# Gated mix of sliding-window attention and a Mish MLP on one core: the softmax in two halves, the gate's sums on VectorE, two chunks of the first projection pass by pass, and the causal bound added by GpSimd

## The chip, the core and the metric

The kernel runs on one core of a Trainium2 chip. A core has TensorE (PE, matrix multiply into PSUM), VectorE (DVE), ScalarE (ACT), GpSimd (POOL) and SyncE (SP, which here issues all DMA transfers). They run beside each other and are tied by semaphores; each works through its own instructions in order. The metric is the device time of one execution in microseconds. Before the change it is 655.41 us (median of three runs, 655.38 to 655.86).

## The reference: what is computed

x has 2048 rows of 640 numbers, all in f32. There are 32 heads of 20, a window of eight keys two rows apart, and an MLP of width 1728:

```
g    = sigmoid(sum(x * gate_w))                                    one number a row
q,k,v = x @ wqkv, in 32 heads
o    = softmax(q . k[row - 0, -2, ..., -14] * 20**-0.5) . v        keys before row 0 count as -1e9
a    = o @ wo
b    = mish(x @ w1 + b1) @ w2
out  = g * a + (1 - g) * b
```

## The kernel before: tiling, stages, order

**Matmuls in three parts.** Every f32 operand is split into a high half (ScalarE, L309) and a low half (a subtraction on VectorE or GpSimd, L312; "ANY" lets either take it). Three matmuls, high by high, high by low and low by high (L343 to L345), replace one f32 matmul. A split operand lives in a "pair" buffer; there are 21 of them, given out in a fixed order, and 14 of the 20 x chunks, wq, w2 and the MLP's activations share them. Raw loads go through seven "raw" and four "hb" buffers; three "w" buffers hold w1.

**Rows and units.** Row 16p + i sits on partition p in slot i. P = 0 or 1 picks every second slot (eight each), since keys lie two rows apart. Attention goes in eight units u = 2 hq + P: hq is one of four groups of eight heads. For each unit `qkv` (L448) projects eight slots: per slot five chunks of 128 input columns, three matmuls each, 120 matmuls of NCOL columns a unit. The columns are 160 each of q, k and v, 16 of the rest of w1, and in the units with hq = 0 two more that hold gate_w, so 498 columns there and 496 later. ScalarE evacuates a bank with L436 (k and v), L438 (q) and L441 (w1's rest), and in units 0 and 1 with one more copy (L443) of the gate's sum into zt. `make_gates` turns zt into the sigmoid. Unit 0 goes chunk by chunk over its first four slots, as the loads arrive: the three matmuls of slot 0, of slot 1, and so on.

**Attention** (L375) runs on VectorE with k, v and q in SBUF (three stores kvq0 to kvq2, used in turn; unit 7 has kvq2). For pairs of slots 6, 4, 2, 0: the product with eight shifted keys (L380, "qk") and its sum over 20 (L383). Then once for all eight slots: the causal bound by a min with `bound` on partition 0 (L387), maximum (L389), subtraction (L390), Exp on ScalarE (L391, with a table load), sum (L392), reciprocal (L393), times the gate (L394), shares pw (L395). Then for each pair of slots the product with v (L400) and three halving additions (L404, L405, L407), and after each two pairs a transpose (L351) whose result is spilled to DRAM. Keys from other partitions come by two halo copies a unit (L480, DMA). The evacuation of unit u into a store waits until unit u - 2 has freed the slot.

**The MLP.** `mlp1` (15 matmuls a bank) fills TensorE between the units; its Mish output goes to DRAM. `mlp2(tb)`, for four blocks tb of 512 columns, takes fourteen steps fc of 15 matmuls (10 in the last); each step needs one pair of activations, and in mlp2(0) one of w2 as well. The results, times 1 - g, are kept, and `wo_out` adds the attention's output projection at the end.

**What sets the order.** No order is written out by hand. `Plan` records every operation as a task with an engine, an estimated time, a rank (SOON, NEXT, LATER; smaller first), tasks it waits for and buffers it takes; `run` (L88) plays them through and issues each engine's instructions in the order that comes out. A change of any estimate can move instructions. Two rules matter here: VectorE takes an "ANY" split during the score products only if it has been ready for 2 us, and GpSimd takes splits only in stretches after a "qk" product unless a task has rank below 0.

Of the kernel before, what the change touches and what calls it, by code (L numbers as in the profile page):

```python
# [8 lines left out]
F32 = mybir.dt.float32  # L9
# [11 lines left out]
FC = 13  # L21
FR = F - FC * 128
RQ = FR // NQ
NCOL = 3 * QF + RQ + 2
ROW = 2 * QF
BIG = 1e9
WARM = 9
# [157 lines left out]


@with_exitstack
def kernel(ctx: ExitStack, tc: tile.TileContext, x, wq, wo, w1, b1, w2, out):
    nc = tc.nc
    scale = DH ** -0.5  # L190
    V, G, A = nc.vector, nc.gpsimd, nc.scalar
# [104 lines left out]
    def consts_g():  # L296
        for i in range(2):
            G.memset(KV[i][0:1, 0:7], 0.0)

        G.memset(bound, 3e38)  # L300
# [74 lines left out]
    def attention(u, P, hq, ready, gates):  # L375
        kv, q, r = KV[UNIT[u]], Q[UNIT[u]], LATER
        prev = last_att[0]
        for s0 in range(6, -1, -2):
            def mul(s0=s0):
                return V.tensor_tensor(pr, window(kv, s0, 0), q[:, s0:s0 + 2, None, :].to_broadcast([128, 2, W, QF]), op=OP.mult)  # L380

            def red(s0=s0):
                V.tensor_reduce(lg_w[:, s0:s0 + 2], pr.rearrange("p s w (h d) -> p s w h d", d=DH), op=OP.add, axis=AX.X)  # L383

            prev = add("DVE", 2850, mul, [prev] + ready[s0], rank=r, kind="qk")
            prev = add("DVE", 2830, red, [prev], rank=r, kind="qk sum")
        prev = add("DVE", 560, lambda: V.tensor_tensor(lg[0:1, 0:7, :, 0:7], lg[0:1, 0:7, :, 0:7],  # L387
                   bound[:, :, None, :].to_broadcast([1, 7, HQ, 7]), op=OP.min), [prev, cg], rank=r)
        prev = add("DVE", 690, lambda: V.tensor_reduce(mx, lg, op=OP.max, axis=AX.X), [prev], rank=r)  # L389
        prev = add("DVE", 700, lambda: V.tensor_tensor(lg, lg, mx[:, :, :, None].to_broadcast([128, 8, HQ, W]), op=OP.subtract), [prev], rank=r)  # L390
        prev = add("ACT", 630 + 2 * TABLE, lambda: A.activation(lg, lg, AF.Exp, scale=scale), [prev], rank=-1)  # L391
        prev = add("DVE", 690, lambda: V.tensor_reduce(sm, lg, op=OP.add, axis=AX.X), [prev], rank=r)  # L392
        prev = add("DVE", 560, lambda: V.reciprocal(sm, sm), [prev], rank=r)  # L393
        prev = add("DVE", 230, lambda: V.tensor_tensor(sm, sm, gate[:, P, :, None].to_broadcast([128, 8, HQ]), op=OP.mult), [prev] + gates, rank=r)  # L394
        prev = add("DVE", 700, lambda: V.tensor_tensor(pw.rearrange("p s w h -> p s h w"), lg, sm[:, :, :, None].to_broadcast([128, 8, HQ, W]), op=OP.mult), [prev], rank=r)  # L395
        for s0 in range(6, -1, -2):
            def mul(s0=s0):
# [5 lines left out]
            prev = add("DVE", 2850, mul, [prev], rank=r, kind="pv")  # L403
            prev = add("DVE", 1510, lambda: V.tensor_tensor(pr[:, :, 0:4], pr[:, :, 0:4], pr[:, :, 4:8], op=OP.add), [prev], rank=r)  # L404
            prev = add("DVE", 850, lambda: V.tensor_tensor(pr[:, :, 0:2], pr[:, :, 0:2], pr[:, :, 2:4], op=OP.add), [prev], rank=r)  # L405

            prev = add("DVE", 515, lambda s0=s0: V.tensor_tensor(q[:, s0:s0 + 2], pr[:, :, 0], pr[:, :, 1], op=OP.add), [prev], rank=r)  # L407
            if s0 % 4 == 0:
                ot = plan.buf("ot", lambda: at.tile([128, QF // 32, 4, 32], F32, name="ot"))
                prev = add("DVE", 830, lambda s0=s0, ot=ot: turn(ot.t, q[:, s0:s0 + 4], QF // 32), [prev], rank=r, take=[ot])  # L410
                tb = 2 * P + (s0 == 0)
                spilled[tb, hq] = turned_out(lambda tb=tb: o_d[tb][hq * QF:(hq + 1) * QF], lambda ot=ot: ot.t, [prev], [ot])
                for s in range(s0, s0 + 4):
                    freed[u, s] = [prev]
        att_end[u] = prev
        last_att[0] = prev

# [11 lines left out]
    def qkv_part(ps, P, hq, i, kc, n):  # L429
        xs = tuple(X[2 * P + i // 4, kc].t[:, j, (i % 4) * 128:(i % 4 + 1) * 128] for j in range(2))  # L430
        mm3(ps.t[:, :n], xs, tuple(WQ[hq, kc].t[:, j, :n] for j in range(2)), kc == 0, kc == KC - 1)

    def qkv_evac(u, P, hq, i, ps, done):
        kv, q, s = KV[UNIT[u]], Q[UNIT[u]], 4 * (1 - i // 4) + i % 4
        before = freed.get((u - 2, s), []) if u < 7 else [zero2[0]]
# [4 lines left out]
        def rest():  # L440
            A.activation(hx[:, P, i, hq], ps.t[:, 3 * QF:3 * QF + RQ], AF.Copy)  # L441
            if hq == 0:
                A.activation(zt[:, P, s:s + 1], ps.t[:, NCOL - 2:NCOL - 1], AF.Copy)  # L443

        c = add("ACT", 170 * (2 if hq == 0 else 1), rest, [b], rank=SOON, hold=[ps])
        return a, b, c

    def qkv(u, P, hq):  # L448
        n = NCOL if hq == 0 else NCOL - 2
        kv = KV[UNIT[u]]  # L450
        ev = {}
        pss = [ps_buf() for _ in range(8)]
        if u == 0:
            last = warmed
            for kc in range(KC):
                for i in range(4):
                    last = pe_add(3 * mm_ns(n), lambda i=i, kc=kc: qkv_part(pss[i], P, hq, i, kc, n),
                               [last] + X[0, kc].ready + WQ[hq, kc].ready, take=[pss[i]] if kc == 0 else [],
                               hold=[pss[i], X[0, kc], WQ[hq, kc]])
# [24 lines left out]
        if hq == 0:  # L484
            gates[P] = [make_gates(P, [ev[i][2] for i in range(8)])]
        attention(u, P, hq, ready, gates[P])

    hxd = {0: [], 1: []}
    g_done = {}

    def make_gates(P, after):
        def run():
# [190 lines left out]
        X[tb, kc] = load_pair(lambda: x[tb, kc], eng, wide=True, home=x_home[:, i] if i < 6 else None, **k)  # L683

    def wq_in(hq, kc, eng, **k):
        n = NCOL if hq == 0 else NCOL - 2
        WQ[hq, kc] = load_pair(lambda: wq[hq, kc][:, :n], eng, n=n, wide=hq == 0, **k)

    def w1_in(fc, eng="ANY"):
# [7 lines left out]
        x_in(1, kc, "DVE")  # L697
    for fc in range(2):
        w1_in(fc)
    for tb in (2, 3):  # L700
        for kc in range(KC):
            x_in(tb, kc, "ANY")

    todo = [(fc, t) for fc in (0, 1) for t in (0, 1)] + [(fc, t) for fc in (0, 1) for t in (2, 3)]
    todo += [(fc, t) for fc in range(2, 10) for t in range(4)]
# [84 lines left out]
```

## Time and profile before

| | |
|---|---|
| median of the runs | 655.41 us (655.38 to 655.86) |
| profiled execution | 655.15 us |
| its span, first to last instruction | 653.4 us |
| mean granted TensorE clock | 0.999 |
| matmuls | 2869 |
| DMA | 82.35 MB, mean 126 GB/s |

TensorE's stages, by the starts of the first matmul of each:

| stage | starts at, us |
|---|---|
| warm-up matmuls | 1.20 |
| unit 0 | 4.70 |
| mlp1 | 32.50 |
| unit 1 | 59.72 |
| mlp1 | 86.91 |
| unit 2 | 114.14 |
| units 3, 4, 5 | 171.14, 228.14, 285.14 |
| units 6 and 7 | 342.14 |
| mlp2(0) and what follows | 394.94 |

VectorE's first score product of the eight units starts at 33.23, 93.82, 147.66, 210.83, 267.35, 324.04, 383.54 and 460.52 us; its last transpose of attention at 526.05.

How to read it: a row of the timeline is start, duration, engine, line, operation, output and input, shape, count, and in brackets the idle time before it with what ended it. A row of a group has the shape and count, then busy time and mean ns of one, then the idle time in front of the group. A matmul's duration is longer than its pitch, since the next one starts before it ends; the pitch is read from the starts. The 40 slices of the page are 16.3 us each, and a 9 means busy for at least 90% of the slice.

### The profile page before, as it was taken

Reading aid. Unit: us, or ns where it says so; the run is one execution under the profiler, and the core shown is the slowest. Engines: PE = TensorE matmul, PEld = TensorE weight load, DVE = VectorE, ACT = ScalarE, POOL = GpSimd, SP = SyncE. Lnnn points to the kernel's source line nnn. Section 1 sums busy time; section 2 is a strip of 40 time slices with the busy share of each in tenths; the row PEclk is TensorE's granted clock in tenths of the full one; section 3 lists DMA queues with packets and bytes.
Section 4 is the critical chain, followed back from the end, with each engine's and each line's share of the span. In section 5 each row is a group of like instructions: output and inputs, shape, how many; then the busy total and the mean of one; then the engine's idle time right before and its main releaser. Section 6 shows DMA issues by size and latency. Waiting matters only on the chain.

```text
span 653.4 us, 7766 instructions
## 1 busy us (share of the span) xinstructions
PE 647.8 (99%) x2869; PEld 538.1 (82%) x2869; DVE 517.6 (79%) x427; ACT 215.2 (33%) x465; POOL 76.9 (12%) x50
## 2 busy tenths in 40 slices
PE   9999999999999999999999999999999999999997
PEld 6888888888888888888888888788888888888886
DVE  6599989999798989889998989999999945333211
ACT  6744252322324232222324252634123135323000
POOL 3010001001000200000021146000320012311000
PEclk9999999999999999999999999999999999999999
DMA  9963357224123322411332278567425336533222
GB/s 323 291 99 129 81 158 103 61 66 135 71 61 113 102 68 68 130 69 41 98 119 87 63 211 242 168 196 213 156 67 193 85 101 221 181 124 108 81 80 80
DMA packets 55014, 82.35 MB, mean 126 GB/s; under 512 B 8144, under 2 KB 23760, under 8 KB 54976
## 3 DMA queue, kind: packets, MB, share of 16 engines
q1 hardware_dynamic: 54976, 81.86, 42.1%
q8 instruction: 22, 0.36, 0.2%
q14 instruction: 16, 0.13, 0.1%
HBM read 44.94 MB, written 27.80 MB: 111 GB/s over the span
## 4 chain that ended last, share of the span: by engine, by line
PE 93%; DVE 5%; DMA 1%; issue 0%; ACT 0%; SPq 0%; DVEq 0%
PE bank L344 31%; PE bank L345 30%; PE bank L343 30%; DVE pr L380 2%; DVE lg L383 2%; PE bank L598 1%; PE bank L597 1%; DMA hb<-in_w 1%; DVE pair L312 1%; DMA hb<-in_wq 0%; DVE kvq L676 0%; ACT pair L309 0%; DVE mx L389 0%; DVE lg L387 0%; ACT kvq L436 0%
## 5 line engine op out<-in xcount | busy, mean ns | idle before, releaser
L344 PE MATMUL bank<-pair 128*128 128x512 f32 (+2 forms) x432 | 167.2, 387 | 0.3 <-DVE pair L312 0.3
L345 PE MATMUL bank<-pair 128*128 128x512 f32 (+2 forms) x432 | 166.9, 386 | 0.0
L343 PE MATMUL bank<-pair 128*128 128x512 f32 (+2 forms) x432 | 166.8, 386 | 0.0
L380 DVE TENSOR_TENSOR pr<-kvq 128x2560 f32<-128x2560 f32 x32 | 93.2, 2914 | 2.2 <-ACT kvq L436 1.3
L344 PEld LDWEIGHTS bank<-pair 128*128 128x128 f32 x432 | 81.1, 188 | 16.4 <-DVE pair L312 0.7
L343 PEld LDWEIGHTS bank<-pair 128*128 128x128 f32 x432 | 81.1, 188 | 15.7
L345 PEld LDWEIGHTS bank<-pair 128*128 128x128 f32 x432 | 81.2, 188 | 15.5
L383 DVE TENSOR_REDUCE lg<-pr 128x128 f32<-128x2560 f32 x32 | 90.3, 2821 | 1.1
L343 PE MATMUL bank<-pair,w 128*128 128x512 f32 x234 | 91.0, 389 | 0.0
L344 PE MATMUL bank<-pair,w 128*128 128x512 f32 x234 | 91.0, 389 | 0.0
L345 PE MATMUL bank<-pair,w 128*128 128x512 f32 x234 | 91.0, 389 | 0.0
L400 DVE TENSOR_TENSOR pr<-kvq,pw 128x2560 f32<-128x2560 f32 x32 | 90.1, 2815 | 0.8
L344 PE MATMUL bank<-pair,kvq 128*128 128x512 f32 (+2 forms) x196 | 75.9, 387 | 0.2 <-DVE pair L312 0.2
L309 ACT ACTIVATE pair<-raw 128x512 fp32r<-128x512 f32 (+2 forms) x85 | 52.1, 632 | 72.6 <-PE bank L345 54.7
L343 PE MATMUL bank<-pair,kvq 128*128 128x512 f32 (+2 forms) x196 | 75.9, 387 | 0.1
L345 PE MATMUL bank<-pair,kvq 128*128 128x512 f32 (+2 forms) x196 | 75.8, 387 | 0.0
L436 ACT ACTIVATE kvq<-bank 128x320 f32<-128x320 f32 x64 | 28.2, 441 | 129.0 <-PE bank L345 128.9
L508 ACT ACTIVATE hb<-bank,bias 128x512 f32<-128x512 f32 x52 | 35.8, 688 | 105.2 <-PE bank L345 72.4
L312 DVE TENSOR_TENSOR pair<-raw,pair 128x512 fp32r<-128x512 f32 (+2 forms) x64 | 43.4, 694 | 24.6 <-ACT pair L309 24.3
L312 POOL TENSOR_TENSOR w<-raw,w 128x640 fp32r<-128x640 f32 x10 | 20.8, 2079 | 300.0 <-ACT w L309 300.0
L344 PEld LDWEIGHTS bank<-pair,w 128*128 128x128 f32 x234 | 43.9, 188 | 9.1
L345 PEld LDWEIGHTS bank<-pair,w 128*128 128x128 f32 x234 | 43.9, 188 | 9.1
(80 smaller groups left out, 705.8 us busy)
## 6 DMA issues: line engine op xcount, KB each, us to landing
act<-hb SPq DMA_DIRECT2D x52, 256.0 KB, 2.1
raw<-act SPq DMA_DIRECT2D x36, 256.0 KB, 3.3
o<-ot SPq DMA_DIRECT2D x64, 80.0 KB, 2.1
raw<-in_w SPq DMA_DIRECT2D x15, 320.0 KB, 3.0
kvq<-kvq SPq DMA_DIRECT2D x8, 560.0 KB, 4.2
hb<-act SPq DMA_DIRECT2D x16, 256.0 KB, 3.2
raw<-in_wq SPq DMA_DIRECT2D x15, 248.0 KB, 4.4
raw<-in_x SPq DMA_DIRECT2D x14, 256.0 KB, 5.0
```

The lines of the kernel that those rows point to most:

```text
L309: a = add("ACT", act_ns(n), lambda: A.activation(hi(), raw(), AF.Copy), after, rank=rank, take=take, hold=hold)
L312: return (V if e == "DVE" else G).tensor_tensor(lo(), raw(), hi().bitcast(F32), op=OP.subtract)
L343: nc.tensor.matmul(ps, ah, bh, start=first, stop=False)
L344: nc.tensor.matmul(ps, ah, bl, start=False, stop=False)
L345: nc.tensor.matmul(ps, al, bh, start=False, stop=last)
L380: return V.tensor_tensor(pr, window(kv, s0, 0), q[:, s0:s0 + 2, None, :].to_broadcast([128, 2, W, QF]), op=OP.mult)
L383: V.tensor_reduce(lg_w[:, s0:s0 + 2], pr.rearrange("p s w (h d) -> p s w h d", d=DH), op=OP.add, axis=AX.X)
L400: V.tensor_tensor(pr.rearrange("p s w (h d) -> p s w h d", d=DH), vw, pw[:, s0:s0 + 2, :, :, None].to_broadcast([128, 2, W, HQ, DH]), op=O ...
L436: a = add("ACT", 400, lambda: A.activation(kv[:, 7 + s], ps.t[:, QF:3 * QF].rearrange("p (a b) -> p a b", a=2), AF.Copy), [done] + before, ...
L508: a = add("ACT", 610, lambda: A.activation(to(hb.t[:n]), src(), AF.Mish, bias=bias[:n, fc:fc + 1]), done + [bias_in], rank=NEXT, take=[hb] ...
L597: nc.tensor.matmul(pss[dc].t, wh, p.t[:, 0], start=False, stop=False)
L598: nc.tensor.matmul(pss[dc].t, wl, p.t[:, 0], start=False, stop=True)
```

## The change

- **NCOL** is 496 for all units: the two columns of gate_w leave wq, and the copy into zt (L443) leaves ScalarE.
- **The gate's sums**: two new inputs, xt (x with its rows as they are, 128 x 16 x 640) and gw (gate_w). `gate_dots(P)` loads gw once, spread over 128 partitions, and eight slots of xt, into columns of kvq1, and forms each sum by one `tensor_tensor_reduce` on VectorE (rank NEXT). The loads for P = 0 wait for the last x chunk of block 1; those for P = 1 reuse the places of the first eight. Unit 1's evacuation, which writes kvq1, waits for all sixteen sums.
- **Pass by pass**: unit 0's first two chunks go through the four slots three times, first all high by high, then high x by low wq, then low x by high wq; the first pass waits only for the high halves.
- **The softmax in halves**: slots 4 to 7 get bound, maximum, subtraction and Exp after the scores of slots 6, 4 (bound) and 2 (the rest), ahead of scores(0); slots 0 to 3 after that. The shares of slots 0 to 3 are formed after the outputs of slots 4 to 7.
- **The bound** is 0 or -BIG/scale, added to the scores by GpSimd (rank -1) in two operations of 3 and 4 slots on partition 0, in place of VectorE's min.

In the changed kernel's program the lines are L388 and L391 for the scores, L398 for the bound, L404 to L406 and L410 to L413 for the softmax, L419 to L426 for the outputs and L546 for the sums.

```
-        for s0 in range(6, -1, -2):
...
-        prev = add("DVE", 560, lambda: V.tensor_tensor(lg[0:1, 0:7, :, 0:7], lg[0:1, 0:7, :, 0:7],
-                   bound[:, :, None, :].to_broadcast([1, 7, HQ, 7]), op=OP.min), [prev, cg], rank=r)
...
+        def bounded(a, b):
+            b = min(b, 7)
+            return step("POOL", 900, lambda: G.tensor_tensor(lg[0:1, a:b, :, 0:7], lg[0:1, a:b, :, 0:7],
+                        bound[:, a:b, None, :].to_broadcast([1, b - a, HQ, 7]), op=OP.add), [cg], rank=-1)
...
+        scores(6)
+        scores(4)
+        fixed4 = bounded(4, 8)
+        scores(2)
+        e4 = softmax(4, fixed4)
+        scores(0)
+        fixed0 = bounded(0, 4)
+        shares(4, e4)
+        e0 = softmax(0, fixed0)
+        outputs(6)
+        outputs(4)
+        out(4)
+        shares(0, e0)
+        outputs(2)
+        outputs(0)
+        out(0)
...
+    def qkv_pass(pss, kc, a, b, n):
+        for i, ps in enumerate(pss):
+            nc.tensor.matmul(ps.t[:, :n], X[0, kc].t[:, a, i * 128:(i + 1) * 128], WQ[0, kc].t[:, b, :n],
+                             start=a == b and kc == 0, stop=False)
...
+            for kc in range(2):
+                (xh, xl), (wh, wl) = X[0, kc].ready, WQ[0, kc].ready
+                for a, b, w in ((0, 0, [xh, wh]), (0, 1, [wl]), (1, 0, [xl])):
+                    last = pe_add(4 * mm_ns(n), lambda kc=kc, a=a, b=b: qkv_pass(pss[:4], kc, a, b, n), [last] + w, ...
...
+    def gate_dots(P):
+        def at(i):
+            return kvq[1][:, i * D:(i + 1) * D]
+        done = []
+        if P == 0:
+            gw_in.append(dma(lambda: at(0), lambda: gw.to_broadcast([128, D]), X[1, KC - 1].ready[:1], size=327680))
+        for s in range(8):
+            i = 1 + s
+            g = dma(lambda i=i: at(i), lambda s=s: xt[:, 2 * s + P], [dots[s]] if P else X[1, KC - 1].ready[:1], size=327680)
+            done.append(add("DVE", 780, lambda i=i, s=s: V.tensor_tensor_reduce(
+                at(i), at(i), at(0), op0=OP.mult, op1=OP.add, scale=1.0, scalar=0.0, accum_out=zt[:, P, s:s + 1]), [g] + gw_in, rank=NEXT))
+        dots.extend(done)
+        gates[P] = [make_gates(P, done)]
```

More of the change, by code (lines that the diff above doesn't have):

```diff
@@ L23 @@
 RQ = FR // NQ
-NCOL = 3 * QF + RQ + 2
+NCOL = 3 * QF + RQ
 ROW = 2 * QF
@@ L187, with kernel @@
 @with_exitstack
-def kernel(ctx: ExitStack, tc: tile.TileContext, x, wq, wo, w1, b1, w2, out):
+def kernel(ctx: ExitStack, tc: tile.TileContext, x, wq, wo, w1, b1, w2, xt, gw, out):
     nc = tc.nc
@@ L298, in consts_g @@
             G.memset(KV[i][0:1, 0:7], 0.0)
-        G.memset(bound, 3e38)
+        G.memset(bound, 0.0)
         G.affine_select(bound, bound, pattern=[[1, 7], [1, 7]], compare_op=OP.is_ge,
@@ L377, in attention, with step, scores, mul @@
         prev = last_att[0]
-        for s0 in range(6, -1, -2):
-            def mul(s0=s0):
+        def step(eng, ns, fn, after=(), **k):
+            nonlocal prev
+            t = add(eng, ns, fn, [prev] + list(after), **k)
+            if eng == "DVE":
+                prev = t
+            return t
+        def scores(s0):
+            def mul():
                 return V.tensor_tensor(pr, window(kv, s0, 0), q[:, s0:s0 + 2, None, :].to_broadcast([128, 2, W, QF]), op=OP.mult)
-            def red(s0=s0):
+            def red():
@@ L383, in red @@
                 V.tensor_reduce(lg_w[:, s0:s0 + 2], pr.rearrange("p s w (h d) -> p s w h d", d=DH), op=OP.add, axis=AX.X)
-            prev = add("DVE", 2850, mul, [prev] + ready[s0], rank=r, kind="qk")
-            prev = add("DVE", 2830, red, [prev], rank=r, kind="qk sum")
-        prev = add("DVE", 560, lambda: V.tensor_tensor(lg[0:1, 0:7, :, 0:7], lg[0:1, 0:7, :, 0:7],
-                   bound[:, :, None, :].to_broadcast([1, 7, HQ, 7]), op=OP.min), [prev, cg], rank=r)
-        prev = add("DVE", 690, lambda: V.tensor_reduce(mx, lg, op=OP.max, axis=AX.X), [prev], rank=r)
@@ L390, in attention @@
[L390 to L394, printed above, removed]
@@ L395, in attention @@
-        prev = add("DVE", 700, lambda: V.tensor_tensor(pw.rearrange("p s w h -> p s h w"), lg, sm[:, :, :, None].to_broadcast([128, 8, HQ, W]), op=OP.mult), [prev], rank=r)
-        for s0 in range(6, -1, -2):
-            def mul(s0=s0):
+            step("DVE", 2850, mul, ready[s0], rank=r, kind="qk")
+            step("DVE", 2830, red, rank=r, kind="qk sum")
+        def bounded(a, b):
+            b = min(b, 7)
+            return step("POOL", 900, lambda: G.tensor_tensor(lg[0:1, a:b, :, 0:7], lg[0:1, a:b, :, 0:7],
+                        bound[:, a:b, None, :].to_broadcast([1, b - a, HQ, 7]), op=OP.add), [cg], rank=-1)
@@ new lines, in softmax, with shares @@
+        def softmax(a, after):
+            h = slice(a, a + 4)
+            step("DVE", 400, lambda: V.tensor_reduce(mx[:, h], lg[:, h], op=OP.max, axis=AX.X), [after], rank=r)
+            step("DVE", 420, lambda: V.tensor_tensor(lg[:, h], lg[:, h], mx[:, h, :, None].to_broadcast([128, 4, HQ, W]), op=OP.subtract), rank=r)
+            return step("ACT", 360 + 2 * TABLE, lambda: A.activation(lg[:, h], lg[:, h], AF.Exp, scale=scale), rank=-1)
+        def shares(a, after):
+            h = slice(a, a + 4)
+            step("DVE", 400, lambda: V.tensor_reduce(sm[:, h], lg[:, h], op=OP.add, axis=AX.X), [after], rank=r)
+            step("DVE", 330, lambda: V.reciprocal(sm[:, h], sm[:, h]), rank=r)
+            step("DVE", 180, lambda: V.tensor_tensor(sm[:, h], sm[:, h], gate[:, P, h, None].to_broadcast([128, 4, HQ]), op=OP.mult), gates, rank=r)
+            step("DVE", 640, lambda: V.tensor_tensor(pw[:, h].rearrange("p s w h -> p s h w"), lg[:, h], sm[:, h, :, None].to_broadcast([128, 4, HQ, W]), op=OP.mult), rank=r)
@@ L398, in mul, with outputs @@
+        def outputs(s0):
+            def mul():
                 vw = window(kv, s0, 1)
@@ L401, in mul, with out @@
                                 pw[:, s0:s0 + 2, :, :, None].to_broadcast([128, 2, W, HQ, DH]), op=OP.mult)
[L403 to L414, printed above, removed]
+            step("DVE", 2850, mul, rank=r, kind="pv")
+            step("DVE", 1510, lambda: V.tensor_tensor(pr[:, :, 0:4], pr[:, :, 0:4], pr[:, :, 4:8], op=OP.add), rank=r)
+            step("DVE", 850, lambda: V.tensor_tensor(pr[:, :, 0:2], pr[:, :, 0:2], pr[:, :, 2:4], op=OP.add), rank=r)
+            step("DVE", 515, lambda: V.tensor_tensor(q[:, s0:s0 + 2], pr[:, :, 0], pr[:, :, 1], op=OP.add), rank=r)
+        def out(s0):
+            ot = plan.buf("ot", lambda: at.tile([128, QF // 32, 4, 32], F32, name="ot"))
+            step("DVE", 830, lambda: turn(ot.t, q[:, s0:s0 + 4], QF // 32), rank=r, take=[ot])
+            tb = 2 * P + (s0 == 0)
+            spilled[tb, hq] = turned_out(lambda: o_d[tb][hq * QF:(hq + 1) * QF], lambda: ot.t, [prev], [ot])
+            for s in range(s0, s0 + 4):
+                freed[u, s] = [prev]
+        scores(6)
[14 more added lines that the diff above has]
+        out(0)
         att_end[u] = prev
@@ L438, in qkv_evac @@
         b = add("ACT", 280, lambda: A.activation(q[:, s], ps.t[:, :QF], AF.Copy), [a], rank=SOON, hold=[ps])
[L440 to L445, printed above, removed]
+        c = add("ACT", 170, lambda: A.activation(hx[:, P, i, hq], ps.t[:, 3 * QF:3 * QF + RQ], AF.Copy), [b], rank=SOON, hold=[ps])
         return a, b, c
     def qkv(u, P, hq):
-        n = NCOL if hq == 0 else NCOL - 2
+        n = NCOL
         kv = KV[UNIT[u]]
@@ L454, in qkv @@
             last = warmed
-            for kc in range(KC):
+            for kc in range(2):
+                (xh, xl), (wh, wl) = X[0, kc].ready, WQ[0, kc].ready
+                for a, b, w in ((0, 0, [xh, wh]), (0, 1, [wl]), (1, 0, [xl])):
+                    last = pe_add(4 * mm_ns(n), lambda kc=kc, a=a, b=b: qkv_pass(pss[:4], kc, a, b, n), [last] + w,
+                                  take=pss[:4] if (kc, a, b) == (0, 0, 0) else [], hold=pss[:4] + [X[0, kc], WQ[0, kc]])
+            for kc in range(2, KC):
                 for i in range(4):
                     last = pe_add(3 * mm_ns(n), lambda i=i, kc=kc: qkv_part(pss[i], P, hq, i, kc, n),
-                               [last] + X[0, kc].ready + WQ[hq, kc].ready, take=[pss[i]] if kc == 0 else [],
+                               [last] + X[0, kc].ready + WQ[hq, kc].ready,
                                hold=[pss[i], X[0, kc], WQ[hq, kc]])
@@ L483, in qkv @@
         hxd[P].extend(ev[i][2] for i in range(8))
-        if hq == 0:
-            gates[P] = [make_gates(P, [ev[i][2] for i in range(8)])]
         attention(u, P, hq, ready, gates[P])
@@ L699 @@
         w1_in(fc)
+    gate_dots(0)
     for tb in (2, 3):
```

13 lines of the change are left out of this document (8 added, 5 removed).

## The prediction

> **What bounds the kernel now.** I read the page's busy times first, then TensorE's waits, then the timeline of TensorE around each wait and at the borders of its stages.
>
> ```profile
> PE 647.8 (99%) x2869; PEld 538.1 (82%) x2869; DVE 517.6 (79%) x427; ACT 215.2 (33%) x465; POOL 76.9 (12%) x50
> ...
> PE   9999999999999999999999999999999999999997
> DVE  6599989999798989889998989999999945333211
> ```
> TensorE is busy in every slice from the first to the last; VectorE is nearly full until slice 32.
>
> ```profile
> PE bank L291 <- DVE lg L287: 1.2, 1, 1.2
> PE bank L344 <- DVE pair L312: 0.5, 2, 0.3
> ```
> These are all of TensorE's waits: the start, and twice a low half (L312). So the time is the sum of matmul pitches plus these few gaps, and nothing on another engine counts until it makes TensorE wait. Starts (first column) give the pitches:
>
> ```profile
> 4.70 0.50 PE L343 MATMUL bank<-pair,kvq 128*128 128x498 f32 x1
> 5.42 0.50 PE L344 MATMUL bank<-pair,kvq 128*128 128x498 f32 x1 [0.22 <-DVE pair L312]
> 5.75 0.39 PE L345 MATMUL bank<-pair,kvq 128*128 128x498 f32 x1
> ...
> 59.72 0.38 PE L343 MATMUL bank<-pair 128*128 128x498 f32 x1
> ...
> 86.91 0.39 PE L343 MATMUL bank<-kvq,w 128*128 128x512 f32 x1
> ...
> 114.14 0.38 PE L343 MATMUL bank<-pair,kvq 128*128 128x496 f32 x1
> ...
> 140.54 0.39 PE L343 MATMUL bank<-kvq,w 128*128 128x512 f32 x1
> ...
> 418.74 0.39 PE L343 MATMUL bank<-pair 128*128 128x512 f32 x1
> 419.44 0.50 PE L344 MATMUL bank<-pair 128*128 128x512 f32 x1 [0.31 <-DVE pair L312]
> 419.78 0.40 PE L345 MATMUL bank<-pair 128*128 128x512 f32 x1
> ```
> The 120 matmuls of unit 1 take 86.91 - 59.72 = 27.19 us (226.6 ns each, 498 columns); those of unit 2 take 140.54 - 114.14 = 26.40 us (220.0 ns, 496 columns). 120 with 512 columns, from 86.91 to 114.14, take 27.23 us (226.9 ns). So 498 columns cost as much as 512.
>
> **The change, part by part.** The sum goes against the profiled execution, 655.15 us (span 653.4). The program order of the changed kernel has the same 2869 matmuls in the same stages, so TensorE's time changes by pitches and gaps only.
>
> 1. *Two columns fewer* in units 0 and 1: 2 x (27.19 - 26.40) = **-1.58 us**. Both widths are in this trace, so I take it whole.
>    [...]
>
> 2. *Pass by pass* in chunks 0 and 1. Now the second matmul waits for wq's low half: starts 4.70, 5.42, 5.75 instead of two pitches, 1.05 - 0.45 = 0.60 us lost. Afterwards four high x high matmuls go first (4.70 to about 5.7), and the low half of wq (VectorE 4.68 to 5.36) is there. A longer first interval remains (0.33 after a restart here, 0.34 after the one at 419.44): **-0.49 us**, bounds 0 and -0.60. What is late next: chunk 1's wq high half ends on ScalarE at 7.06 and is wanted at 4.70 + 0.10 + 12 x 0.22 = 7.4; its low half ends at 7.77, wanted at 8.3. Nothing.
>
> 3. *The middle gap*: 418.74, 419.44, 419.78 is 1.04 - 0.45 = 0.59 us; the matmul stood behind a split that VectorE did only after the mul at 415.95. In the new order VectorE makes thirteen splits after three score pairs of unit 6, before its softmax, where now it makes five after four. **-0.58 us**, bounds 0 and -0.58. It holds if unit 6 is in time (next part).
>
> Sum: 655.15 - 1.58 - 0.49 - 0.58 = 652.5; the median shown is 0.26 above the profiled execution, so **652.8**.
>
> 4. *The rest, costed at nothing*, because it lies on engines beside TensorE. Prices from these rows (mean ns, then idle before):
>
> ```profile
> L312 DVE TENSOR_TENSOR w<-raw,w 128x640 fp32r<-128x640 f32 x5 | 4.1, 824 | 2.6 <-ACT w L309 2.5
> L389 DVE TENSOR_REDUCE mx<-lg 128x64 f32<-128x512 f32 x8 | 5.5, 686 | 0.3
> L392 DVE TENSOR_REDUCE sm<-lg 128x64 f32<-128x512 f32 x8 | 5.5, 686 | 12.8 <-ACT lg L391 12.8
> L387 DVE TENSOR_TENSOR lg<-lg,bound 1x392 f32<-1x392 f32 x8 | 5.2, 653 | 0.3
> L493 DVE TENSOR_SCALAR zt<-zt 128x8 f32<-128x8 f32 x2 | 0.3, 147 | 0.0
> ```
> - *Sixteen gate sums.* No such operation is in the trace. The program has two instructions for each: low bound a 640-wide tensor_tensor plus the smallest operation, 824 + 147 = 0.97 us; high bound with a 640-wide reduce behind it (686 x 640/512 = 858), 1.83 us. I take 1.0, 16 us in all, as it is one instruction over one stream.
>   [...]
> - *Softmax in halves*, per unit: widths 640 (824) and 512 (692) give about 1.03 ns a column and 0.16 fixed, so the six split operations gain six fixed parts, some 0.9 us at most; I take 0.4. Off go the min (0.65) and the waits for Exp (12.8 us over seven units), since Exp of one half now lies beside scores(0) (5.7 us) or two outputs.
> - *The -BIG on GpSimd*, 16 times, 168 or 224 elements: its 512-wide tensor_tensor takes 1.29 alone, 3.4 at most beside VectorE, so 0.4 to 3.4 us. The first half is covered by scores(2) (5.7 us), the second by the first half's shares (1.7 us). Without cover the softmax behind it waits up to 1.7 us a unit, VectorE time. Beside GpSimd's splits the muls at L380 took 3.45 instead of 2.83; a GpSimd add may stretch one so, 0.6 us a unit.
> - *Loads*: 17 x 320 KB, 5.6 MB; DMA moved 307 GB/s in the first 33 us, so 18 us of it. On SP's queue eight stand ahead of unit 0's halo copy, all of them behind the last X load (16.90 us), so no matmul waits; about 7.2 MB stand before them (25 us), the first eight sums end near 36.5, and unit 0's scores start then instead of 33.23. Seventeen issues of 0.33 to 0.45 us are not felt.
> - *ScalarE* loses 16 copies of zt (3.3 us). Exp waits in its order in front of evacuations; eight banks cover over 20 us. Unit 1's evacuation now waits for the last sum: 36.5 + 17.7 (scores, gates) + 8 = 62, first bank full near 61; TensorE would want the banks back only from about 74.
>
> Does VectorE's delay reach TensorE? It resynchronises wherever splits wait for pair buffers that TensorE gives back:
>
> ```profile
> 88.09 3.19 DVE L312 TENSOR_TENSOR pair<-raw,pair 128x496 fp32r<-128x496 f32 x5 [2.99 <-ACT pair L309]
> ...
> 382.93 0.69 DVE L312 TENSOR_TENSOR pair<-raw,pair 128x512 fp32r<-128x512 f32 x1 [2.98 <-ACT pair L309]
> 383.54 2.82 DVE L380 TENSOR_TENSOR pr<-kvq 128x2560 f32<-128x2560 f32 x1
> ```
> These five splits are released by unit 1's last matmul (2.1 us earlier afterwards). In the new order they stand in the middle of unit 0's outputs, so 16.3 us of unit 0 come after them: unit 1 starts near 105.5 (now 93.82). A unit is 52.8 us of its own work plus splits of w. Going on so with releases near 196.7, 310.7 and 380.9, the starts are 159, 217, 270, 329 and, for unit 6, 389.7 (now 147.66, 210.83, 267.35, 324.04, 383.54). VectorE still arrives early at the four releases, by 1.4, 0.4, 2.3 and 2.2 us, 6.3 together.
>   Unit 6 is the tight place. mlp2(0) starts near 392.9 and takes a pair for w2 and one for act every 3.4 us. Pairs 11 to 13 are GpSimd's, behind its add, which waits for two score pairs: number 12 is ready at unit 6's start + 11.4 + 1 + 2 x 2.1 = 406.3, wanted at 409.9. So 3.5 us are left; beyond 6.3 + 3.5 = **9.8 us** of extra VectorE time, TensorE loses 1 us per us. No later place is nearer: the last spill is wanted after 600.
>
> **The rivals.**
> - *The sums at their high bound* (1.83): 13.8 us more, 4.0 beyond the cover: 656.7; between, anything from 653. For: it writes its products and keeps a running sum as well, which no row prices. Against: it reads each stream once.
> - *Slower: unit 6 starts too late.* If the sums also run beside loads and GpSimd as L380 did (3.45/2.83 = 1.22), 2.23 us each are 19.7 us more; unit 6 starts near 403, and mlp2(0) stands 9.9 us: about 662. It decides from a start at 393, and is slower by over 0.2% from 397. For: VectorE is 92% busy from 94 to 460 us. Against: four idle stretches to eat first.
> - *The middle gap stays*: 653.4. For: loads of the pairs still wait on each other. Against: thirteen splits before the softmax.
> - *The pitch does not fall*: 652.8 + 1.58 = 654.4. Against: unit 2's 220.0 ns. [...]
>
> **How the numbers follow.** The forecast (652.2 to 653.2) 0.58; the middle gap or another gap under a microsecond (to 654.1) 0.08; the pitch 0.02; the sums at their high bound (654.1 to 656.7) 0.12; unit 6 late 0.20. A measurement of this kernel tells about 0.2% (1.3 us) from no change: faster 0.66, same 0.14, slower 0.20. The range 652.1 to 656.7 leaves the last case out.
>
> **What would show it.** Right: the first 120 matmuls at 220 ns; starts near 4.70, 5.03, 5.25; no wait of TensorE on L312; unit 1's first score near 105 and unit 6's near 390; no VectorE wait for Exp; sums near 1.0 us. Wrong: TensorE waiting for pairs between 400 and 430, sums of 1.6 us or more, or a TensorE wait for a bank near 80 us.

## The result and the profile after

| kernel | median, us | range, us | ratio to before |
|---|---|---|---|
| before | 655.39 | 655.31 to 655.87 | 1 |
| after | 653.21 | 652.86 to 653.73 | 0.9965 [0.9952, 0.9978] |

The changed kernel is 2.2 us faster; the forecast was 652.8, with a range of 652.1 to 656.7. Its profiled execution took 653.41 us (span 651.6, mean granted clock 1.000), 1.74 us less than the one of before.

The page of the changed kernel, its busy times and two rows of the 40 slices:

```profile
PE 646.8 (99%) x2869; PEld 538.5 (83%) x2869; DVE 528.3 (81%) x501; ACT 214.1 (33%) x457; POOL 96.5 (15%) x64
...
PE   9999999999999999999999999999999999999997
DVE  5779899999997999999899979999999965333211
```
VectorE is busy for 10.7 us longer than before (528.3 against 517.6) in a shorter time, and TensorE is as full as it was. That is the first thing to see: the engine whose work was rearranged has more to do, not less.

TensorE's waits in the changed kernel (total, times, longest):

```profile
PE bank L291 <- DVE lg L287: 1.2, 1, 1.2
```
Only the wait at the very start is left; both waits on L312 are gone. The starts of its stages, and the three matmuls that stood before at 418.74, 419.44 and 419.78, now in a run of even starts:

```profile
4.88 1.67 PE L474 MATMUL bank<-pair,kvq 128*128 128x496 f32 x4
...
59.53 0.38 PE L343 MATMUL bank<-pair 128*128 128x496 f32 x1
...
85.93 0.39 PE L343 MATMUL bank<-kvq,w 128*128 128x512 f32 x1
...
113.13 0.38 PE L343 MATMUL bank<-pair,kvq 128*128 128x496 f32 x1
...
417.73 0.39 PE L343 MATMUL bank<-pair 128*128 128x512 f32 x1
417.96 0.39 PE L344 MATMUL bank<-pair 128*128 128x512 f32 x1
418.19 0.39 PE L345 MATMUL bank<-pair 128*128 128x512 f32 x1
```
Unit 1 takes 85.93 - 59.53 = 26.40 us, 220.0 ns a matmul, where it took 27.19. Unit 0 goes from 4.88 to 32.30 (the first matmul of mlp1), 27.42 us where it took 27.80. From 113.13 to the start of the last matmul (647.57) pass 534.44 us; before, from 114.14 to 649.22, it was 535.08. The 0.64 between them is the middle gap (0.58) and 0.06 besides. So the gains add up to 0.38 (unit 0) + 0.79 (unit 1) + 0.64, less 0.18 for the later start (4.88 against 4.70): 1.63 of the 1.65 us by which the last matmul starts earlier.

VectorE's groups with new or changed shapes (count, busy time and mean ns, then idle time before them):

```profile
L546 DVE CUSTOM_DVE_ANT_0 kvq<-kvq 128x640 f32<-128x640 f32 x16 | 13.7, 904 | 0.0
L546 DVE DVE_READ_ACCUMULATOR2_ANT zt<- 128x1 f32 x16 | 1.3, 80 | 0.0
L388 DVE TENSOR_TENSOR pr<-kvq 128x2560 f32<-128x2560 f32 x32 | 91.2, 2852 | 2.1 <-DMA kvq<-kvq 1.5
L410 DVE TENSOR_REDUCE sm<-lg 128x32 f32<-128x256 f32 x16 | 6.3, 392 | 0.0
```
A gate sum is two instructions, 0.90 and 0.08 us. The sums of a half (L410) wait for nothing, where the whole softmax waited 12.8 us for Exp. And where VectorE arrives early, the releases that the prediction used:

```profile
87.11 3.13 DVE L312 TENSOR_TENSOR pair<-raw,pair 128x496 fp32r<-128x496 f32 x5 [0.73 <-ACT pair L309]
...
197.71 3.13 DVE L312 TENSOR_TENSOR pair<-raw,pair 128x496 fp32r<-128x496 f32 x5 [2.79 <-ACT pair L309]
...
311.71 1.96 DVE L312 TENSOR_TENSOR pair<-raw,pair 128x496 fp32r<-128x496 f32 x3 [2.43 <-ACT pair L309]
...
381.05 1.29 DVE L312 TENSOR_TENSOR pair<-raw,pair 128x512 fp32r<-128x512 f32 x2 [4.01 <-ACT pair L309]
```
The brackets hold 0.73, 2.79, 2.43 and 4.01 us in which VectorE stood with nothing to do: its additional work fitted ahead of each of them.

### The profile page after: what moved, and what is told of

Same layout as the page of the kernel before. It is cut to its first block, busy times and chain, and to the rows that moved or that the text cites. A ratio compares the mean times of both kernels' runs of the same rounds, so it can differ in the third digit from the quotient of the medians.

```text
span 651.6 us, 7877 instructions
## 1 busy us (share of the span) xinstructions
PE 646.8 (99%) x2869; PEld 538.5 (83%) x2869; DVE 528.3 (81%) x501; ACT 214.1 (33%) x457; POOL 96.5 (15%) x64
## 3 DMA queue, kind: packets, MB, share of 16 engines
HBM read 50.50 MB, written 27.80 MB: 120 GB/s over the span
## 4 chain that ended last, share of the span: by engine, by line
PE 99%; DVE 0%; issue 0%
PE bank L344 32%; PE bank L345 32%; PE bank L343 32%; PE bank L474 1%; PE bank L657 1%; PE bank L658 1%; PE bank L291 1%; DVE kvq L736 0%; DVE lg L287 0%
## 5 line engine op out<-in xcount | busy, mean ns | idle before, releaser
L345 PE MATMUL bank<-pair 128*128 128x496 f32 (+1 forms) x432 | 166.6, 386 | 0.0
L343 PE MATMUL bank<-pair 128*128 128x496 f32 (+1 forms) x432 | 166.6, 386 | 0.0
L344 PE MATMUL bank<-pair 128*128 128x496 f32 (+1 forms) x432 | 166.6, 386 | 0.0
L388 DVE TENSOR_TENSOR pr<-kvq 128x2560 f32<-128x2560 f32 x32 | 91.2, 2852 | 2.1 <-DMA kvq<-kvq 1.5
L419 DVE TENSOR_TENSOR pr<-kvq,pw 128x2560 f32<-128x2560 f32 x32 | 90.4, 2824 | 0.8
L391 DVE TENSOR_REDUCE lg<-pr 128x128 f32<-128x2560 f32 x32 | 90.2, 2819 | 0.9
L309 ACT ACTIVATE pair<-raw 128x512 fp32r<-128x512 f32 (+1 forms) x85 | 52.2, 630 | 70.8 <-PE bank L345 47.9
L345 PE MATMUL bank<-pair,kvq 128*128 128x512 f32 (+1 forms) x188 | 72.6, 386 | 0.0
L344 PE MATMUL bank<-pair,kvq 128*128 128x512 f32 (+1 forms) x188 | 72.6, 386 | 0.0
L343 PE MATMUL bank<-pair,kvq 128*128 128x512 f32 (+1 forms) x188 | 72.6, 386 | 0.0
L480 ACT ACTIVATE kvq<-bank 128x320 f32<-128x320 f32 x64 | 28.1, 439 | 119.2 <-PE bank L345 119.2
L312 DVE TENSOR_TENSOR pair<-raw,pair 128x512 fp32r<-128x512 f32 (+1 forms) x67 | 45.2, 695 | 23.3 <-ACT pair L309 23.2
L343 PEld LDWEIGHTS bank<-pair,w 128*128 128x128 f32 x234 | 43.9, 188 | 9.2
L345 PEld LDWEIGHTS bank<-pair,w 128*128 128x128 f32 x234 | 43.9, 188 | 9.1
L344 PEld LDWEIGHTS bank<-pair,w 128*128 128x128 f32 x234 | 43.9, 188 | 9.1
```

Of the source, the lines that this page charges most:

```text
L309: a = add("ACT", act_ns(n), lambda: A.activation(hi(), raw(), AF.Copy), after, rank=rank, take=take, hold=hold)
L312: return (V if e == "DVE" else G).tensor_tensor(lo(), raw(), hi().bitcast(F32), op=OP.subtract)
L343: nc.tensor.matmul(ps, ah, bh, start=first, stop=False)
L344: nc.tensor.matmul(ps, ah, bl, start=False, stop=False)
L345: nc.tensor.matmul(ps, al, bh, start=False, stop=last)
```

## The experiments

Two theories. **A**, the prediction's: the time is the sum of TensorE's pitches and gaps; VectorE, GpSimd and ScalarE count only where TensorE stops. **B**, the rival: the change pays by what it takes from VectorE's chain (the waits for Exp, the bound), and loses by what it puts there (the sums).

The kernels ran in three rounds, each with the one before beside them: 655.53 us with e1 to e4, 655.43 with e5 to e8, 655.47 with e9 to e11. "Gaps" is what TensorE's starts in the profiled execution show above the pitch after the first 8 us, and "less gaps" is the median without them. The intervals of the ratios reach 0.6 to 0.8 us to either side, so a difference of some tenths is read from TensorE's starts; the medians alone don't show it.

| kernel | median, us | ratio to before | gaps, us | less gaps |
|---|---|---|---|---|
| before | 655.43 to 655.53 | 1 | 0.58 | 654.85 to 654.95 |
| e1_cols: columns alone | 653.72 | 0.9975 [0.9965, 0.9984] | 0.05 | 653.67 |
| e2_pass: passes alone | 654.60 | 0.9987 [0.9978, 0.9995] | 0 | 654.60 |
| e3_halves: halves and bound alone | 654.92 | 0.9992 [0.9983, 1.0001] | 0.11 | 654.81 |
| e4_whole: all but the halves | 654.86 | 0.9992 [0.9983, 1.0001] | 1.58 | 653.28 |
| e11_nopass: all but the passes | 655.66 | 1.0004 [0.9995, 1.0013] | 2.29 | 653.37 |
| e5_free: all, sums nearly free | 653.32 | 0.9966 [0.9953, 0.9978] | 0 | 653.32 |
| e6_sums2: all, sums doubled | 652.87 | 0.9961 [0.9948, 0.9973] | 0 | 652.87 |
| e8_after: the change as it is | 653.27 | 0.9966 [0.9954, 0.9979] | 0 | 653.27 |

**e1_cols**, the two columns alone (the gate's sum is left out):

```
-NCOL = 3 * QF + RQ + 2
+NCOL = 3 * QF + RQ
...
-            if hq == 0:
-                A.activation(zt[:, P, s:s + 1], ps.t[:, NCOL - 2:NCOL - 1], AF.Copy)
...
+        G.memset(zt, 0.0)
```


> The kernel before with 496 columns in units 0 and 1 and nothing else; the gate's sum is left out (zeros in zt). Theory A (the time is TensorE's pitches and gaps): unit 1 falls by 0.79 us as unit 2 showed; unit 0 falls by 0.79 at 220.0 ns, or only by 0.40 if its pitch is the 223.3 ns that the changed kernel showed there. So 653.8 to 654.2, with the middle gap and the start as before. Theory B (VectorE's relief from the waits for Exp is what pays): no change, 655.4.

It measured 653.72, and in its profile the middle gap is gone too, although nothing of attention was touched. Less gaps, the columns bring 1.2 to 1.3 us (654.85 or 654.95 less 653.67), not 1.58. Unit 1 runs at 220.0 ns; unit 0 begins at 220 and, after one interval of 273 ns at 8.2 us, runs at 223.3.

**e2_pass**, the passes alone:

```
-            for kc in range(KC):
+            for kc in range(2):
+                (xh, xl), (wh, wl) = X[0, kc].ready, WQ[0, kc].ready
+                for a, b, w in ((0, 0, [xh, wh]), (0, 1, [wl]), (1, 0, [xl])):
+                    last = pe_add(4 * mm_ns(n), lambda kc=kc, a=a, b=b: qkv_pass(pss[:4], kc, a, b, n), [last] + w, ...
+            for kc in range(2, KC):
```


> The kernel before with chunks 0 and 1 of unit 0 pass by pass and nothing else. Theory A as predicted: 0.49 us off, 654.9. Rival A2 (seen in the changed kernel's trace, where the first intervals were 580, 413 and 290 ns although nothing was waited for): TensorE is still at a slow clock when the first real matmuls start, so the passes gain 0.1 us or nothing in such a run; 655.3. The intervals of the first 24 matmuls tell. Theory B: 655.4.

It measured 654.60, 0.83 to 0.93 us better, of which 0.58 are the middle gap, which vanished here as well; 0.25 to 0.35 are left for the passes. Its first starts are 0.58, 0.41, 0.41 and 0.23 us apart: nothing was waited for, but the first matmuls ran at half the pace.

**e3_halves**, softmax in halves and the bound on GpSimd alone:

```
-        for s0 in range(6, -1, -2):
-            def mul(s0=s0):
...
+        scores(6)
+        scores(4)
+        fixed4 = bounded(4, 8)
+        scores(2)
+        e4 = softmax(4, fixed4)
...
```


> The kernel before with the softmax in halves and the bound on GpSimd, and nothing else. Theory A: only the middle gap can go, 654.8, and nothing if the new order leaves it or another. VectorE's waits for Exp (12.8 us) go. Theory B: the whole gain of the change is here, 653.2.

It measured 654.92, 0.5 to 0.6 us better (the interval of the ratio just includes no change). TensorE's starts show the middle gap gone and a new one of 0.11. Taking the waits for Exp out of VectorE's chain brought nothing beyond that, against theory B.

**e4_whole**, the changed kernel with the softmax whole and the min back on VectorE:

```
-        e4 = softmax(4, fixed4)
...
+        prev = add("DVE", 560, lambda: V.tensor_tensor(lg[0:1, 0:7, :, 0:7], lg[0:1, 0:7, :, 0:7],
+                   bound[:, :, None, :].to_broadcast([1, 7, HQ, 7]), op=OP.min), [prev, cg], rank=r)
...
```


> The changed kernel with the softmax whole again, as before: columns, passes and the sums on VectorE stay. Theory A: the waits for Exp come back and VectorE runs later, which costs nothing unless a pair is late for mlp2(0); the order in that stretch is another (many splits ahead of unit 6), so 653.2, to 654.2 with a gap in mlp2. Theory B: 16 us of sums and 12.8 us of waits without relief, 655.4 or more.

It measured 654.86, 1.6 us worse than the changed kernel, and TensorE's starts hold it all. From its timeline:

```profile
517.07 0.39 PE L343 MATMUL bank<-pair 128*128 128x512 f32 x1
518.07 0.50 PE L344 MATMUL bank<-pair 128*128 128x512 f32 x1 [0.61 <-DVE pair L312]
...
573.78 0.39 PE L345 MATMUL bank<-pair,w 128*128 128x512 f32 x1
574.19 0.50 PE L343 MATMUL bank<-pair,kvq 128*128 128x512 f32 x1
574.53 0.40 PE L344 MATMUL bank<-pair,kvq 128*128 128x512 f32 x1
575.05 0.50 PE L345 MATMUL bank<-pair,kvq 128*128 128x512 f32 x1
```
From 517.07 to 518.07 is 0.77 us more than a pitch, with 0.11 more behind it: TensorE waits for a split of VectorE's. The four starts from 573.78 to 575.05 hold 0.6, with 0.1 behind. There a load is late, as the rows of ScalarE and VectorE show:

```profile
573.40 0.74 ACT L309 ACTIVATE kvq<-raw 128x640 fp32r<-128x640 f32 x1 [5.26 <-DMA raw<-in_wo]
574.17 0.83 DVE L312 TENSOR_TENSOR kvq<-raw,kvq 128x640 fp32r<-128x640 f32 x1 [5.70 <-ACT kvq L309]
```
Both engines stood idle for over 5 us until this part of wo had landed. Its load was issued at 569.06, while the changed kernel issues its last load of wo at 561.40. So the halves are worth something only because the order that comes out with the softmax whole is late in two places, once with a split and once with a load.

**e5_free**, **e6_sums2** and **e7_sums3**, the changed kernel in its order, with each sum replaced by a one-column operation (e5), or with one or two more products of 640 columns behind each sum (e6, e7):

```
+            def sums(i=i, s=s):
                 V.tensor_tensor_reduce(at(i), at(i), at(0), ..., accum_out=zt[:, P, s:s + 1])
+                for _ in range(1):
+                    V.tensor_tensor(at(i), at(i), at(0), op=OP.mult)
```


> The changed kernel, every engine's order kept, with each gate sum replaced by an operation on one column (the sums are left out, the loads stay): about 12 us less VectorE work in 33 to 63 us. Theory A: no change (653.2, within 0.3), and unit 6's first score at the same 390, since it waits for pair buffers. Theory B: faster by some us.

> The changed kernel, order kept, with a second 640-wide operation behind each sum: 13.1 us more on VectorE. The prediction said that 9.8 us are covered, so 3.3 us would be lost: 656.5. By the idle time that the changed kernel's trace shows in front of the releases (0.7 + 2.8 + 2.4 + 4.0) and some 3.3 at the pairs of mlp2(0), 13.2 are covered: 653.2 to 653.7. Theory B: 13 us more, or a good part of it, 660 and above.

> As the run before, with two more operations behind each sum: 26.2 us more on VectorE. Beyond the cover TensorE should lose one us per us: by the prediction's 9.8 us 16.4 lost, 669.6; by 13.2 of the trace 13 lost, 666.2. If the time stays near 653, the price of one us per us is wrong.

Without the sums' time: 653.32. With sixteen more products (13.1 us at 0.82 each; VectorE's busy time is 11.7 us above the changed kernel's): 652.87, no wait of TensorE, and unit 6's first score at 388.50 (389.98 in the changed kernel). VectorE's time on this path is worth nothing either way, which theory B can't explain. With 32 more products: 664.94 (ratio 1.0151 [1.0136, 1.0167]), but not where I had put the tight place. The waits of e7_sums3 that the changed kernel doesn't have, and TensorE around the first:

```profile
PE bank L343 <- ACT hx L484: 7.3, 1, 7.3
PE bank L345 <- POOL w L312: 2.1, 1, 2.1
```
```profile
81.92 0.38 PE L345 MATMUL bank<-pair 128*128 128x496 f32 x1
89.64 0.78 PE L343 MATMUL bank<-pair 128*128 128x496 f32 x1 [7.34 <-ACT hx L484]
90.22 0.61 PE L344 MATMUL bank<-pair 128*128 128x496 f32 x1
```
It is a wait for a bank, which the prediction named only as a sign ("a TensorE wait for a bank near 80 us"). ScalarE's rows in the same kernel show why:

```profile
77.68 0.44 ACT L480 ACTIVATE kvq<-bank 128x320 f32<-128x320 f32 x1 [21.09 <-DVE kvq L549]
78.14 1.28 ACT L561 ACT_TABLE_LOAD   x1
86.02 0.21 ACT L561 ACTIVATE zt<-zt 128x8 f32<-128x8 f32 x1 [6.59 <-DVE zt L547]
88.90 0.28 ACT L482 ACTIVATE kvq<-bank 128x160 f32<-128x160 f32 x1
```
ScalarE is idle for 21 us ahead of the first evacuation of unit 1 (L480), which one of the added products (L549) releases when it has left its place in kvq1. Then the gate's Exp (L561) stands in ScalarE's order ahead of the other evacuations and waits 6.59 us more for the last sum. TensorE, behind its matmul at 81.92, finds no bank free for its next slot.

**e8_after**, the change again:

> The changed kernel once more, for its start: Theory A2 says that the moment at which TensorE's clock comes up differs from execution to execution, so the first intervals differ from 580, 413 and 290 ns here; unit 0's later pitch is again 223.3 ns if it belongs to the kernel, 220.0 if to the execution. Time 653.2 within 0.4.

It measured 653.27, and its profiled execution 652.88, 0.53 less than the first one. Both have no gap; the whole difference lies before mlp1's first matmul (31.75 against 32.30). TensorE's first intervals in e8_after are 0.33 and 0.23 us, where the first execution had 0.58, 0.41 and 0.29; unit 0's later pitch is 223.3 ns again.

**e9_mul4** and **e10_mul2**, the changed kernel with VectorE's work lengthened just ahead of unit 6:

```
             def mul():
+                for _ in range(4 if (u, s0) == (5, 6) else 0):
+                    V.tensor_tensor(pr, window(kv, s0, 0), q[:, s0:s0 + 2, None, :].to_broadcast([128, 2, W, QF]), op=OP.mult)
                 return V.tensor_tensor(pr, window(kv, s0, 0), ...
```


> The changed kernel, every engine's order kept; in unit 5 the score product of slots 6 and 7 is made five times over in place of once (the same values each time), so VectorE has 4 x 2.82 = 11.3 us more to do just before unit 6, after all earlier waits have been eaten. It tests the tight place that the prediction names. By theory A (the cover ends at unit 6): 4.0 us of it vanish in VectorE's wait ahead of the splits at 381 us; the other 7.3 us move unit 6's start from 390.0 to about 396.7 to 397.3. The pair that GpSimd splits behind its add (at 405.06 to 406.3 now, at about 413 then) is wanted by TensorE at 410.9, so TensorE stops for 2 to 4 us between 405 and 420 us, waiting for pair, L312, on POOL: 655.3 to 657.3 us. If the cover at unit 6 is larger than read: 653.3, no wait. If VectorE's time counted one for one: 664.6.

> As the run with five products, with three: 2 x 2.82 = 5.6 us more on VectorE just before unit 6. By theory A 4.0 us of it vanish in the wait at 377 to 381 us, 1.6 us move unit 6's start to about 391 to 391.6, and GpSimd's pair, ready at about 408, is still ahead of 410.9: 653.3 us, no wait of TensorE. If VectorE's time counted one for one: 658.9.

e9_mul4 measured 659.59 (658.77 to 659.85; ratio 1.0058 [1.0042, 1.0073]), 6.3 us more than the changed kernel, where 2 to 4 were expected; e10_mul2 654.00 (653.05 to 654.61; 0.9972 [0.9962, 0.9983]). Unit 6 starts at 396.85 (396.7 to 397.3 expected) and at 391.85 (391 to 391.6 expected). TensorE in e9_mul4, GpSimd's rows, and windows around the stop (the column behind the busy time is the granted clock):

```profile
410.45 0.39 PE L343 MATMUL bank<-pair 128*128 128x512 f32 x1
414.01 0.50 PE L344 MATMUL bank<-pair 128*128 128x512 f32 x1 [3.17 <-POOL pair L312]
...
432.50 0.39 PE L343 MATMUL bank<-pair 128*128 128x512 f32 x1
434.42 0.50 PE L344 MATMUL bank<-pair 128*128 128x512 f32 x1 [1.52 <-DVE pair L312]
```
```profile
408.32 3.18 POOL L400 TENSOR_TENSOR lg<-lg,bound 1x168 f32<-1x168 f32 x1 [6.24 <-DVE lg L393]
411.47 1.26 POOL L312 TENSOR_TENSOR pair<-hb,pair 128x512 fp32r<-128x512 f32 x1
```
```profile
405.00:410.40 5.40, 5.40 (x25) 1.00 0.82 258
410.40:414.00 3.60, 0.44 (x2) 1.00 0.24 68
414.00:417.80 3.80, 3.79 (x10) 0.58 0.72 226
```
The predicted tight place is there: the pair behind GpSimd's add, and a stop of 3.3 us where 2 to 4 were expected. What was not expected is another 3.5 in the profiled execution (659.85). After the stop the clock is granted at 0.58 for 3.8 us and eight starts are 0.40 to 0.43 us apart instead of 0.227 (1.6 us). And there is a second stop, 1.8 us, at a place that I had not seen. e10_mul2 reaches that place alone; its TensorE and its VectorE there:

```profile
428.38 0.39 PE L343 MATMUL bank<-pair 128*128 128x512 f32 x1
428.85 0.50 PE L344 MATMUL bank<-pair 128*128 128x512 f32 x1
```
```profile
428.11 0.69 DVE L312 TENSOR_TENSOR pair<-raw,pair 128x512 fp32r<-128x512 f32 x1
```
A single split stands behind the second half's subtraction (L407 here) and ends at 428.80; the matmul that reads it starts at 428.85, 0.24 late. In the changed kernel that split ends at 427.86 and is wanted at 428.16: the margin there is 0.3 us, the smallest that these runs found. The gap costs 0.35 in all, and the start of this execution another 1.02 (mlp1's first matmul at 32.77, at 31.75 in e8_after's profiled execution): 652.88 + 0.35 + 1.02 = 654.25, and its profiled execution measured 654.26.

**e11_nopass**, the changed kernel with chunks 0 and 1 slot by slot again:

```
-            for kc in range(2):
-                (xh, xl), (wh, wl) = X[0, kc].ready, WQ[0, kc].ready
...
-            for kc in range(2, KC):
+            for kc in range(KC):
```


> The changed kernel with unit 0's first two chunks slot by slot again, as before the change; the rest stays. The planner's order of VectorE and GpSimd moves a little with it. If the prediction's second term is right, TensorE's second matmul waits again for wq's low half (a wait on L312 of 0.2 to 0.5 us at 5 us) and the time is 0.3 to 0.6 us longer than the changed kernel's 653.2: 653.5 to 653.9. Its rival is that the slow clock of the first matmuls sets their pace anyway, so that the wait is hidden: 653.2, no difference. A new gap of TensorE, up to 0.6 us, can come with the new order.

It measured 655.66, 2.4 us worse, outside what either side expected. The first matmuls do wait again (first column):

```profile
4.74 0.70 PE L343 MATMUL bank<-pair,kvq 128*128 128x496 f32 x1
5.45 0.49 PE L344 MATMUL bank<-pair,kvq 128*128 128x496 f32 x1
5.78 0.39 PE L345 MATMUL bank<-pair,kvq 128*128 128x496 f32 x1
...
424.38 0.39 PE L343 MATMUL bank<-pair 128*128 128x512 f32 x1
425.98 0.50 PE L344 MATMUL bank<-pair 128*128 128x512 f32 x1 [1.21 <-POOL pair L312]
...
472.39 0.39 PE L343 MATMUL bank<-pair 128*128 128x512 f32 x1
473.31 0.50 PE L344 MATMUL bank<-pair 128*128 128x512 f32 x1 [0.53 <-POOL pair L312]
```
But mlp1 starts at 32.14, earlier than in the first execution of the changed kernel (32.30). The loss is at 424.38 (1.60 - 0.23 = 1.37, and 0.11 behind it) and at 472.39 (0.70 and 0.11), 2.29 us, 400 us after the edit. Without the passes the planner deals the splits around unit 6 in another order, and GpSimd gets two of them late.

## Why the prediction was right, and where its steps were off

- **What bounds the kernel.** Right. Theory A holds in all kernels: the time follows TensorE's starts, and about 12 us less or more of VectorE's busy time (e5_free, e6_sums2) moved nothing.
- **1, two columns fewer (-1.58).** Right mechanism, mis-sized: unit 1 gave 0.79 as priced, at 220.0 ns. Unit 0's matmuls settled at 223.3 ns rather than 220.0 in most executions (220.0 in e5_free), which takes 0.4 off; e1_cols measured 1.2 to 1.3.
- **2, pass by pass (-0.49).** In the profiled pair this is the largest miss. I priced the wait of one execution against a TensorE at its full pace. With 496 columns, unit 0's first 120 matmuls take 27.40 and 27.42 us slot by slot (e11_nopass, e1_cols); pass by pass they take 26.91 to 27.00 in five executions, so 0.4 to 0.5 less, about as priced. In three more they take 27.41, 27.50 and 28.06, with starts 0.41 apart until the clock came up at 6.0 to 7.1 us. In every slot-by-slot execution it had come up by 5.3, so what the passes are worth under a later clock is not shown. The medians gave 0.25 to 0.35 (e2_pass) and 0.1 to 0.2 less gaps (e11_nopass), too little to tell from 0.49. The starts that I named as a sign (4.70, 5.03, 5.25) came in their intervals in e8_after (4.84, 5.17, 5.40), not in the first execution (4.88, 5.46, 5.88).
- **3, the middle gap (-0.58).** It went, as priced, but my reason was not needed: it went in e1_cols and e2_pass as well, whose softmax is whole. Every new plan removed this gap, and some made others.
- **The sum.** -2.65 was said for the profiled execution and 652.8 for the median; measured were -1.74 and 653.2. The 0.9 in the profiled pair are 0.4 of term 1, 0.5 of term 2 and 0.18 of a later start (4.88 for 4.70), less 0.15 from unit 2 on and behind the last matmul. So 652.8 came within 0.4 us although two terms were too large; the range held them.
- **4, the rest at nothing.** Right. A sum took 0.90 + 0.08 us in the mean (1.0 said), and where sums follow each other they start 0.75 us apart, since the two overlap (a sum's second instruction and the next sum both start at 28.99). Most sums take 0.82 us, as long as a plain 640-wide tensor_tensor (0.82 to 0.83); two that ran beside an operation on GpSimd took 1.87 (at 47.69) and 1.16 (at 52.97). GpSimd's add took 0.65 to 3.19, within 0.4 to 3.4 (the most that I read for a 512-wide one, 3.4, was too low: one took 3.89 before the change). The first eight sums ended at 34.3 (36.5 said), the last at 63.3 (62).
- **VectorE's course.** Unit starts 105.5, 159, 217, 270, 329, 389.7 were said; 106.08, 159.15, 218.52, 272.12, 328.37, 389.98 measured. The stops ahead of releases came to 10.0 us in place of 6.3.
- **The cover.** Two parts failed. "No later place is nearer" is wrong: a split at 427.17 ends 0.3 us ahead of its matmul, against about 4 at the place that I named (in e9_mul4 unit 6 is 7.4 us later against mlp2(0), and the stop is 3.3). And "1 us per us" is too little: the stop of 3.3 cost 5.0 with the slow clock behind it (granted at 0.58). For work put into the sums the cover is larger than 9.8 (sixteen more products, 11.7 us of busy time, cost nothing) and ends at unit 1's banks, not at unit 6.
- **The rivals.** The sums at their high bound (656.7) fell by the measured 0.9; even 1.8 a sum costs nothing (e6_sums2). My price for them was off as well: from the 1.0 that I had taken, 1.83 is 13.3 us more, not 13.8, so 656.3. Unit 6 too late is a real mechanism in this order, and it decides near where I said, 393: a start at 391.85 (e10_mul2) lost 0.4 us, at another place, and one at 396.85 (e9_mul4) made the kernel 0.6% slower than before, where I had said 0.2%. But the sums don't bring it there. Nor is the start alone what decides: in e4_whole, whose order of splits is another, unit 6 starts at 419.69 and TensorE doesn't stop before 517. The middle gap and the pitch are answered above.

Left open: why unit 0's pitch at 496 columns is 223.3 ns in all profiled executions but e5_free's, where it is 220.0 as in the later units.

## What to carry to other kernels

Where one engine is 99% busy, sum its starts: pitches, gaps, and nothing else; an edit elsewhere is worth what it moves there. When a planner deals the work, any edit can open or close gaps far from it (0 to 2.3 us here, as large as the whole gain), so price an edit with its gaps taken off, and expect the gaps to come out anew. A margin is found by listing every split with the matmul that reads it, not by following the chain that looks tightest.

## What the runs showed of the hardware

- **The clock at the start.** The first matmuls run 0.43 us (512 columns) and 0.413 us (496) apart, nearly double the later pitch, until a moment that differs between the 13 profiled executions, 3.9 to 7.1 us, and between two of one program (6.0 and 4.2 in the changed kernel's). The trace's record of the granted clock begins at that moment (before the change at 3.88 us, where the starts go from 0.43 to 0.22 us apart); the views count the time before it as 1.00. The same 0.41 us between starts comes back in e7_sums3 at a granted clock of 0.50. Between 4.6 and 6.5 us e8_after starts seven matmuls of unit 0 and e10_mul2 four:

```profile
4.84 1.83 PE L474 MATMUL bank<-pair,kvq 128*128 128x496 f32 x7
...
4.71 2.16 PE L476 MATMUL bank<-pair,kvq 128*128 128x496 f32 x4
```
  I take it for most of the spread of 652.86 to 653.73: in the four gapless profiled executions of this order (the changed kernel's two, e5_free, e6_sums2), whose times are 652.86 to 653.49, the time less the start of mlp1's first matmul is 621.09 to 621.13.
- **The clock after a stop.** After stops of 7.5 us (e7_sums3) and 3.3 us (e9_mul4) the starts were 0.40 to 0.43 us apart for some 4 us (behind a first interval of 0.58 and 0.34), at a granted clock of 0.50 (89.6 to 93.6 us) and 0.58 (414.0 to 417.8); after 2.3 us (e7_sums3's second), 1.7 us (e9_mul4's second) and less (e11_nopass) a single interval was 0.34 and the next 0.23. The two long stops cost 2.0 and 1.7 us more than their length.
- **GpSimd's add on one partition.** These are the two shapes of the bound in the changed kernel:

```profile
L398 POOL TENSOR_TENSOR lg<-lg,bound 1x168 f32<-1x168 f32 x8 | 22.9, 2868 | 25.3 <-DVE lg L391 25.3
L398 POOL TENSOR_TENSOR lg<-lg,bound 1x224 f32<-1x224 f32 x8 | 5.2, 649 | 56.1 <-DVE lg L391 56.1
```
The smaller takes four times as long. Seven of its eight run beside a score product on VectorE (L388) and take 3.11 to 3.19 us; the eighth, at 52.46 beside a gate sum, took 0.99. The larger runs beside small operations of the softmax. All eight of the smaller end 0.40 to 0.41 us after the end of the product or sum beside which they start: they last as long as what is left of that instruction, and 0.4 us more. So the add on the tight path to unit 6's pairs ends 0.4 us behind VectorE's score product (401.91 to 405.09, the product from 401.87 to 404.70); why it ends only then, these runs don't show.
